# Sketched attention and a squared-ReLU FFN on one core: another order for the first batch, remainders of q through DRAM, k's outer products on GpSimd

## The chip, the cores and the metric

The kernel runs on one core of one Trainium2 chip. Its engines are TensorE (PE, with its weight loads PEld), VectorE (DVE), ScalarE (ACT), GpSimd (POOL) and SyncE (SP, which issues DMAs only). The metric is the device time of one execution in microseconds, as a median of several runs.

## The reference

Attention with polynomial sketched features, without a softmax, and then a feed-forward block with a squared ReLU on its output:

```python
# q, k, v: (4, 4, 1088, 32) float32; S1, S2: (8, 32)
def phi(x):
    a = np.einsum('rd,bhsd->bhsr', S1, x)
    b = np.einsum('rd,bhsd->bhsr', S2, x)
    return np.einsum('bhsi,bhsj->bhsij', a, b).reshape(*x.shape[:-1], 64)
q_p, k_p = phi(q), phi(k)
kv = np.einsum('bhsf,bhsd->bhfd', k_p, v)
z = np.sum(k_p, axis=2)
num = np.einsum('bhsf,bhfd->bhsd', q_p, kv)
den = np.einsum('bhsf,bhf->bhs', q_p, z)[..., None] + 1e-06
x = (num / den).transpose(0, 2, 1, 3).reshape(4352, 128)
h = np.maximum(x @ w_in, 0.0)            # w_in: (128, 2048)
out = h * h @ w_out                      # w_out: (2048, 128)
```

## The kernel before

There are four batches (`b`) of 1088 tokens and four heads. A batch is cut into two groups (`g`) of 512 tokens and a remainder of 64. The tokens of a group become one chunk of the FFN (8 chunks of 512 tokens); the remainders of all four batches together are the ninth chunk, of 256 tokens. For each chunk, the hidden size 2048 is taken in 16 blocks. A block is one product `pg` (f16, line 857), a ReLU into `gt`, a square into `g2`, and one product into `po` (f32, line 944). `first_product` (line 843) makes the first half up to three blocks ahead, `block` (line 923) does the second. The ReLU is done by DVE and the square by ACT (lines 873 and 876), or the ReLU by ACT and the square by GpSimd (lines 864 and 865), or both by ACT (lines 870 and 871); `first_product` chooses by counters.

The order of all instructions is written out by hand. The attention of a batch is cut into Python generators ("lanes") that `pump` (line 797) advances between blocks; `now` counts blocks. Counters such as `pool_free`, `quiet` and `ms_until` say from which block on an engine or a PSUM bank is taken to be free. When a chunk is asked for that isn't there yet, `first_product` sets `hurry` and drives all lanes until it is.

For a batch b >= 1, `batch_gen` (line 665) transposes k and q on DVE (`turned`), projects them on TensorE (`proj_rests`, `proj4`), and has the outer products `ph_k` of k's two factors made (`outer`, line 314): in two steps, group 0 on DVE, group 1 on GpSimd, then the remainder's on GpSimd (`outer_rest`). `KvRows` sums k's features against v, `spread` puts the sums into `kvbd`. The features of q take another way: the factors `qf` are stored to a DRAM scratch (`q_rows`) and read back by DMAs that repeat rows (`factors_gen`, line 272), and one GpSimd multiplication of two such tiles `f` gives the transposed features `phT` (line 300). `x_gen` (line 639) makes the numerators and denominators of a group (`numerators`, into the two PSUM banks of `nd`, each group of 256 columns filled up to 132), normalizes them on DVE, transposes the result on TensorE (`x_ps`) and copies it as the chunk `xT`. `second_gen` (line 720) does the second group.

For the remainder of q, GpSimd makes the outer products `phr_q`, TensorE transposes them (`rest_features_t`, line 748, `tr_ps`), and `rest_numerators` (line 762) makes their numerators in a bank of its own (`ndr`). `rest_x` (line 773) normalizes the remainders of two batches at a time.

Batch 0 is done ahead of the first block, from line 953 on. Its q features are transposed on TensorE (`feature_t`): those of group 0 before the first block, those of group 1 (`phq1`, outer products on DVE at line 1003) after the first two `pg`; group 1's numerators come from the lane `first_gen`. `idle_products` are matrix products of zeros into an unused bank. `sum_constants` (line 206) makes small constants on DVE. v comes in four DMAs per batch, each for 32 partitions and all four heads (`load_v`, line 110).

The last chunk is stored from two PSUM tiles by rows (`rows_store`, line 911), with four DMAs each on SP and ACT in turn; the products of the second tile's last three blocks are held back until the first is stored.

Of the kernel before, what the change touches and what calls it, by code (L numbers as in the profile page):

```python
# [21 lines left out]
def kernel(  # L22
# [19 lines left out]
    E = 128  # L42
# [67 lines left out]
    def load_v(b, i, eng):  # L110
        eng.dma_start(
            _v(v_sb[b], 0, [[256, H], [1, 256]], 32 * i, 32),
            bass.AP(
                v.tensor,
                v.offset + (b * H * S + 8 * i) * D,
                [[NM * D, 32], [S * D, H], [1, 256]],
            ),
        )
# [87 lines left out]
    def sum_constants():  # L206
        dve.tensor_reduce(
            out=pick_s[:, :], in_=_v(iden, 0, [[1, 32], [32, 4]]), axis=AX, op=add
        )
        dve.tensor_copy(  # L210
            out=_v(pick, 0, [[8, 32], [1, 8]]), in_=_v(pick_s, 0, [[1, 32], [0, 8]])
        )
        dve.tensor_reduce(
            out=_v(own_j, 0, [[8, 2], [1, 8]]),
            in_=_v(iden, 0, [[64, 2], [1, 8], [8, 8]]),
            axis=AX,
            op=add,
        )
# [53 lines left out]
    def factors_gen(b, qf, phT):  # L272
# [5 lines left out]
        for g in range(2):  # L278
            for pr in range(2):
# [16 lines left out]
                phT[g].append(fs)  # L296

# [33 lines left out]
    rest_ab = {}  # L331
    for r in range(2):
        rest_ab[r] = (
            cpool.tile([128, 128], F32, name=f"abr{r}"),
            {x: cpool.tile([128, 256], F32, name=f"phr_{x}{r}") for x in "kq"},
        )

    def proj_rests(items, ps_tag="ms"):

        ab_ps = pspool.tile([128, 128], F32, name="abr_ps", tag=ps_tag, bufs=2)  # L340
        for xt, b, kind in items:
            tiled(ab_ps, 64 * "kq".index(kind), 64, xt, 0, w_bd[:, :], 64, 64 * (b % 2))
        for xt, b, kind in items:
            p0, x = 64 * (b % 2), "kq".index(kind)
            if kind == "q" and any(y[1:] == (b, "k") for y in items):
                continue
            m = 8 if any(y[1:] == (b, "q") for y in items) and kind == "k" else 4
            act.copy(
                _v(rest_ab[b // 2][0], 32 * x, [[64, 2], [8, m], [1, 8]], p0, 64),
                _v(ab_ps, 64 * x, [[8, 2], [16, m], [1, 8]], p0, 64),  # L350
            )

    def outer_rest(b, kind, eng):
        p0, c0 = 64 * (b % 2), 32 * "kq".index(kind)
        ab, ph = rest_ab[b // 2]
        eng.tensor_tensor(
            out=_v(ph[kind], 0, [[64, 4], [8, 8], [1, 8]], p0, 64),
            in0=_v(ab, c0, [[8, 4], [1, 8], [0, 8]], p0, 64),
            in1=_v(ab, c0 + 64, [[8, 4], [0, 8], [1, 8]], p0, 64),
# [3 lines left out]
    class Kv:  # L363
# [25 lines left out]
        def rest(self):  # L389
            r, p0 = self.b // 2, 64 * (self.b % 2)  # L390
            self.products(rest_ab[r][1]["k"], 0, v_rm[r], 0, D, H * D, p0, 64)
# [10 lines left out]
    class KvRows:  # L402
# [26 lines left out]
        def products(self, phs):  # L429
# [11 lines left out]
            self.values(rest_ab[r][1]["k"], 0, v_rm[r], 0, D, p0, 64, False, True)  # L441
            self.factors(rest_ab[r][0], 0, 64, 0, p0, 64, False, True)
# [69 lines left out]
    def normalize(nd, T, xT, col, parts=1):  # L512
# [61 lines left out]
        for i in range(0, T, m):  # L574
            ms_used()
            x_ps = pspool.tile([128, 512], F16, name="x_ps", tag="ms", bufs=2)
# [34 lines left out]
    wanted = [-9]  # L611
    shared = [0]

    def pool_time(blocks):

        pool_free[0] = max(pool_free[0], now[0] + 0.7) + blocks
        return int(pool_free[0] - now[0]) + 1

# [20 lines left out]
    def x_gen(b, g, phT, rests=()):  # L639

        yield from take_nd()
        while pool_free[0] > now[0] + 0.6 and not hurry[0]:
            yield 1, 0
        nd = numerators(b, phT)
# [4 lines left out]
        yield next(norm)  # L649
        yield next(norm)  # L650
        next(norm)
        yield 1, 0
        nd_taken[0] = False
        for u in rests:
            rest_numerators(u)
        yield 1, 0
# [8 lines left out]
    def batch_gen(b):  # L665
# [3 lines left out]
        for x, sb in (("k", k_sb), ("q", q_sb)):  # L669
            if x == "q":  # L670
                yield from not_before(4 if b == 1 else n0 - 39)
            for g in range(2):
                xt[x, g] = turned(sb[b], g)
                yield 1, 1
        rests = [(turned(sb[b], 2), b, x) for x, sb in (("k", k_sb), ("q", q_sb))]
        if b == 1:
            rests.append((turned(q_sb[0], 2), 0, "q"))
        yield 1, 0
        yield from not_before(n0 - 28)
# [6 lines left out]
        lanes.insert(0, [factors_gen(b, qf, phT), now[0] + 1, 0])  # L686
        n1 = now[0]
        wanted[0] = n1 + 8
# [3 lines left out]
        for t0 in (0, 2):  # L692
            outer(phk[0], ab_k, t0, 2, dve, None, 0)
            outer(phk[1], ab_k, t0, 2, pool, None, 1)
            pool_time(1.0)
            yield 1, 1
        yield from pool_ready(1.0)
        outer_rest(b, "k", pool)
# [3 lines left out]
        while now[0] < ready and not hurry[0]:  # L702
# [10 lines left out]
            [second_gen(b, phT, n1, [x[1] for x in rests if x[2] == "q"]), n1 + 10, 0]  # L713
# [6 lines left out]
    def second_gen(b, phT, n1, rests):  # L720
        for u in rests:
            yield from pool_ready(1.0)
            outer_rest(u, "q", pool)
            pool_time(0.6)
            yield 1, 0
        yield from pool_ready(0)
        yield from ms_both()
        for u in rests:
            rest_features_t(u)
        yield 1, 0  # L730
        while 2 * b not in chunks:
            yield 1, 0
        yield from features_gen(b, phT, 1, n1 + 14)
        yield 1, 0
# [3 lines left out]

    def first_gen(phT):
        yield from x_gen(0, 1, phT)  # L740
# [7 lines left out]
    def rest_features_t(b):  # L748
        p0 = 64 * (b % 2)
        ph = rest_ab[b // 2][1]["q"]  # L750
        ms_used()
        t_ps = pspool.tile([128, 512], F32, name="tr_ps", tag="ms", bufs=2)
        for pr in range(2):
            nc.tensor.transpose(
                t_ps[:, 64 * pr : 64 * pr + 64],
                ph[p0 : p0 + 64, 128 * pr : 128 * pr + 128],
                iden[p0 : p0 + 64, p0 : p0 + 64],
            )
        phT_rem[b] = apool.tile([128, 128], F32, name="phTr", tag="phTr", bufs=2)
        act.copy(phT_rem[b][:, :], t_ps[:, 0:128])  # L760

    def rest_numerators(b):
        p0 = 64 * (b % 2)
        ms_used()
        nd = pspool.tile([128, 512], F32, name="ndr", tag="ms", bufs=2)
        for pr in range(2):
            tiled(
                nd, 2 * VW * pr, 2 * VW, phT_rem[b], 64 * pr,
                kvbd[b][:, 2 * VW * pr : 2 * VW * pr + 2 * VW], 64, p0,
            )  # L770
        act.copy(nd_rem[b // 2][p0 : p0 + 64, :], nd[p0 : p0 + 64, 0 : 4 * VW])

    def rest_x(r):
        beta = yield from normalize(nd_rem[r], 1, xT_rem, 128 * r)
        rem_beta.append((beta, 1))
        for w in range(2):
            for i in range(2):
                dst = bass.AP(
                    out.tensor,
                    out.offset + ((2 * r + w) * S + 32 + i) * E,  # L780
                    [[NM * E, 32], [1, E]],
                )
                rem_dst.append((dst, 64 * w + 32 * i, 32, 128 * r, 128))
# [30 lines left out]
    def store_gen(po, nt, betas, dsts):  # L814
# [7 lines left out]
        for t in range(T):  # L822
            nc.tensor.transpose(  # L823
                o_ps[:, 128 * t : 128 * t + 128], oT[:, 128 * t : 128 * t + 128], iden[:, :]
            )
        o_sb = fpool.tile([128, 512], F32, tag="o_sb", bufs=2)
# [16 lines left out]
    def first_product():  # L843
# [16 lines left out]
        calm = now[0] >= quiet[0] and not wanted[0] - 2 <= now[0] <= wanted[0] + 1  # L860
# [8 lines left out]
        elif now[0] == quiet[0] - 2 and nt == 512:  # L869
            act.activation(gt[:, 0:nt], pg[:, 0:nt], Relu)  # L870
            act.activation(g2[:, 0:nt], gt[:, 0:nt], Square)
        else:
            dve.tensor_scalar(  # L873
# [37 lines left out]
    def rows_store(r, ci):  # L911
# [8 lines left out]
        for i, (dst, p0, n, _, w) in enumerate(chunks[ci][3][4 * r : 4 * r + 4]):  # L920
            (sp, act)[i % 2].dma_start(dst, _v(o_sb, 0, [[1, w]], p0, n))

    def block():
# [6 lines left out]
        if nt < 512:  # L930
# [3 lines left out]
            if c < NC - 3:  # L934
# [34 lines left out]
    proj_rests([(xk[2], 0, "k")])  # L969
    phk = [ph_tile("ph_k", 3) for g in range(2)]  # L970
# [4 lines left out]
    xq = turned(q_sb[0], 0)  # L975
    idle_products(4)
    pq = proj(xq)
    outer_rest(0, "k", dve)
# [88 lines left out]
```

## Time and profile before

| what | value |
|---|---|
| median of 3 runs | 202.36 us (202.26 to 202.84) |
| the profiled execution | 202.01 us, of which the span is 200.2 us |
| granted TensorE clock | 0.998 |
| first `pg` starts | 17.86 us |
| a block without other work, start to start of `pg` | 1.07 to 1.08 us |
| DVE ReLU, 128x512 (L873) | 0.685 us, x92 |
| ACT square, 128x512 (L876) | 0.630 us, x92 |
| GpSimd square, 128x512 (L865) | 1.041 us, x27 |
| k's outer product 128x512, DVE / GpSimd in b >= 1 (L321) | 1.04 us / 1.27 us |
| GpSimd multiplication of q's factors (L300) | 1.276 us, x12 |
| remainder's outer product of q, GpSimd (L356) | 0.624 us, x4 |

All times below are of the one profiled execution, in microseconds from the start of its span. A row of the timeline gives start, length, engine, line, operation and tiles; in brackets stands how long the engine was idle before it and what released it. Rows that follow each other on one engine and line are merged (x2). In the chain of waits each piece is what held up the next, back from the last instruction. Matrix products are pipelined, so TensorE counts as busy across short waits; the starts of the `pg` products show them better than its busy share.

### The profile page before, as it was taken

How to read it: one execution, taken by the hardware profiler on the slowest of the kernel's cores; microseconds unless marked ns; L12 is line 12 of the kernel's file. 1: busy time of each engine (PE TensorE's matmuls, PEld its weight loads, DVE VectorE, ACT ScalarE, POOL GpSimd, SP SyncE). 2: the span in 40 equal slices, each digit the busy share in tenths (PEclk: the TensorE clock that was granted, in tenths of full speed). 3: DMA queues.
4: the chain of work that ended last, by engine and by line, in shares of the span. 5: the costliest groups of instructions: out<-in, count | busy, mean ns of one | idle time of the engine just before them, and what ended most of it. 6: DMA issues, size and time to landing. Idle time of an engine off the chain costs nothing.

```text
span 200.2 us, 3760 instructions
## 1 busy us (share of the span) xinstructions
PE 193.0 (96%) x1416; PEld 102.8 (51%) x1416; DVE 121.9 (61%) x271; ACT 109.4 (55%) x216; POOL 62.7 (31%) x82
## 2 busy tenths in 40 slices
PE   7798999999999999999999999999999999999992
PEld 2575455455445464564346555454455444444792
DVE  4768694644994717459966573648456844544671
ACT  2236757544565566354674554555647565565570
POOL 3502220844262207441262254331332222223000
PEclk9999999999999999999999999999999999999999
DMA  5999720488300245782000117501000200100021
GB/s 159 279 356 246 229 47 0 137 188 211 111 0 0 66 153 164 210 246 81 2 3 0 52 58 222 194 3 54 0 0 3 52 0 0 38 16 0 3 52 26
DMA packets 14994, 18.34 MB, mean 92 GB/s; under 512 B 3072, under 2 KB 9472, under 8 KB 14976
## 3 DMA queue, kind: packets, MB, share of 16 engines
q1 hardware_dynamic: 14416, 18.00, 32.1%
q8 instruction: 11, 0.18, 0.4%
q10 hardware_dynamic: 560, 0.11, 0.3%
q14 instruction: 7, 0.06, 0.1%
HBM read 15.08 MB, written 3.01 MB: 90 GB/s over the span
## 4 chain that ended last, share of the span: by engine, by line
PE 86%; DVE 6%; DMA 4%; issue 1%; ACT 1%; SPq 0%; DVEq 0%
PE po L944 50%; PE pg L857 15%; PE nd L245 5%; DVE gt L873 2%; DMA v_sb<-in_v_dram 2%; PE kvr_ps L412 2%; PE o_ps L823 2%; PE ab_ps L245 2%; DMA k_sb<-in_k_dram 2%; PE po_r L903 2%; PE po L903 2%; PE idle_ps L224 1%; PE ab_ps L262 1%; PE kv_ps L375 1%; DVE ph_k L321 1%
## 5 line engine op out<-in xcount | busy, mean ns | idle before, releaser
L944 PE MATMUL po<-g,w_o 128*128 128x512 f32 x256 | 130.7, 592 | 0.0
L873 DVE TENSOR_SCALAR gt<-pg 128x512 f32<-128x512 f32 (+1 forms) x108 | 69.1, 646 | 51.7 <-PE pg L857 40.5
L876 ACT ACTIVATE g<-gt 128x512 f32<-128x512 f32 (+1 forms) x108 | 64.2, 599 | 66.0 <-DVE gt L873 63.7
L944 PEld LDWEIGHTS po<-g,w_o 128*128 128x128 f32 x256 | 48.5, 191 | 35.6 <-issue 21.3
L865 POOL TENSOR_TENSOR g<-gt 128x512 f32<-128x512 f32 x27 | 28.1, 1041 | 79.7 <-ACT gt L864 79.5
L857 PE MATMUL pg<-xT,w_in 128*128 128x512 f16 x126 | 47.8, 381 | 0.6 <-DVE gt L873 0.6
L857 PEld LDWEIGHTS <-w_in 128*128 128x128 f16 x142 | 13.9, 98 | 24.0 <-issue 22.8
L300 POOL TENSOR_TENSOR phT<-f,f 128x512 f32<-128x512 f32 x12 | 15.2, 1276 | 8.2 <-DMA f<-q_rows 8.2
L864 ACT ACTIVATE gt<-pg 128x512 f32<-128x512 f32 x27 | 15.9, 588 | 0.0
L321 POOL TENSOR_TENSOR ph_k<-ab 128x512 f32<-128x512 f32 x8 | 9.7, 1236 | 5.9 <-ACT ab L269 4.7
L245 PEld LDWEIGHTS nd<-kvbd,phT 128*64 128x64 f32 x256 | 8.3, 137 | 5.3 <-issue 4.0
L321 DVE TENSOR_TENSOR ph_k<-ab 128x512 f32<-128x512 f32 x6 | 6.2, 1036 | 6.5 <-ACT ab L269 6.5
L245 PE MATMUL nd<-kvbd,phT 128*64 128x66 f32 x256 | 9.5, 225 | 0.2 <-ACT phT L72 0.2
L569 POOL TENSOR_TENSOR beta<-mp 128x4 f32<-128x4 f32 (+1 forms) x10 | 2.1, 206 | 21.0 <-DVE mp L539 21.0
L224 PE MATMUL idle_ps<-zero 128*128 128x512 f16 x23 | 7.1, 455 | 1.2 <-DVE own L185 1.2
L829 DVE TENSOR_TENSOR o_sb<-o_ps,beta 128x512 f32<-128x512 f32 x8 | 5.5, 692 | 4.5 <-PE o_ps L823 2.7
L245 PEld LDWEIGHTS ab_ps<-w_bd,xt 128*64 128x64 f32 x160 | 6.2, 139 | 3.0 <-DVE xt L234 1.5
L245 PE MATMUL ab_ps<-w_bd,xt 128*64 128x64 f32 x160 | 6.4, 225 | 0.8 <-DVE xt L234 0.7
L234 DVE STREAM_TRANSPOSE xt<-k_sb 128x512 f32<-128x512 f32 x8 | 5.5, 698 | 1.7 <-DMA k_sb<-in_k_dram 1.7
L903 PE MATMUL po<-w_o,g 128*128 128x128 f32 x32 | 6.2, 280 | 0.1
L823 PEld LDWEIGHTS o_ps<-iden,oT 128*128 128x128 f32 x32 | 4.0, 141 | 3.7 <-issue 2.9
L903 PE MATMUL po_r<-w_o,g 128*128 128x128 f32 x32 | 5.9, 275 | 0.0
(110 smaller groups left out, 150.8 us busy)
## 6 DMA issues: line engine op xcount, KB each, us to landing
f<-q_rows SPq DMA_DIRECT2D x12, 256.0 KB
f<-q_rows SPq DMA_DIRECT2D x24, 128.0 KB
v_sb<-in_v_dram SPq DMA_DIRECT2D x16, 128.0 KB
out_dram<-o_sb SPq DMA_DIRECT2D x32, 64.0 KB
k_sb<-in_k_dram SPq DMA_DIRECT2D x3, 544.0 KB
q_sb<-in_q_dram SPq DMA_DIRECT2D x3, 544.0 KB
w_in<-in_moe_w_in_dram SPq DMA_DIRECT2D x2, 512.0 KB
w_o<-in_moe_w_out_dram SPq DMA_DIRECT2D x2, 512.0 KB
```

The costliest lines, as they stand in the source:

```text
L224: nc.tensor.matmul(idle_ps[:, :], zero[:, 0:128], zero[:, :])
L245: nc.tensor.matmul(out_ps[p0 + c : p0 + c + z, c0 : c0 + w], lhsT[:, l0 + c : l0 + c + z], rhs)
L300: eng.tensor_tensor(out=sb[:, :], in0=fs[0][:, :], in1=fs[1][:, :], op=mult)
L321: eng.tensor_tensor(out=_v(ph, 256 * t0, [[64, 4 * m], [8, 8], [1, 8]]), in0=_v(a, c0, [[n, 4 * m], [1, 8], [0, 8]]), in1=_v(b, c1, [[n, 4 ...
L823: nc.tensor.transpose(o_ps[:, 128 * t : 128 * t + 128], oT[:, 128 * t : 128 * t + 128], iden[:, :])
L857: nc.tensor.matmul(pg[:, 0:nt], w_in[:, 128 * c : 128 * c + 128], xT[:, 0:nt])
L864: act.activation(gt[:, 0:nt], pg[:, 0:nt], Relu)
L865: pool.tensor_tensor(out=g2[:, 0:nt], in0=gt[:, 0:nt], in1=gt[:, 0:nt], op=mult)
L873: dve.tensor_scalar(out=gt[:, 0:nt], in0=pg[:, 0:nt], scalar1=0.0, scalar2=None, op0=amax)
L876: act.activation(g2[:, 0:nt], gt[:, 0:nt], Square)
L903: nc.tensor.matmul(po[r][:, 0:128], g2[:, 128 * r : 128 * r + 128], w_o[:, 128 * c : 128 * c + 128], start=c == 0, stop=c == NC - 1,)
L944: nc.tensor.matmul(po[0][:, 0:nt], w_o[:, 128 * c : 128 * c + 128], g2[:, 0:nt], start=(c == 0), stop=(c == NC - 1),)
```

## The change

The changed kernel computes the same result. In words:

- v comes in one DMA per head over all 128 partitions, four per batch as before.
- Before the first block: `xq` is transposed on DVE ahead of k's outer products, `xq1` after the sums of k; q's group 1 has its outer products on GpSimd, its transposes among the idle products ahead of the first `pg`, its copies on ACT and DVE, and its numerators directly behind the first two `pg`. `x_ps` of the first chunk is taken from the banks of `po`.
- `sum_constants` becomes a lane that starts at block 8, one of its three operations on GpSimd.
- For b >= 1, all four outer products of k are made on GpSimd.
- The remainder of q is projected with the roles of the operands swapped, stored to DRAM (`qr_rows`) and read back in six DMAs; GpSimd multiplies the two tiles. Transposes on TensorE and outer products on GpSimd go. Batch 1 carries two remainders, batches 2 and 3 one each.
- The remainder's numerators go into free columns of the second group's `nd`, ahead of that group's normalization.
- A counter `dve_free` is kept for DVE; transposes, normalization and stores wait in the order until it allows them, and ReLUs go to ACT when it is far ahead. GpSimd takes no squares until nine blocks after the projections (`held_until`). `pump` advances up to nine lanes per block instead of two.
- The last chunk's rows are stored with two DMAs per tile instead of four, and two blocks' products are held back instead of three.

```diff
@@ load_v
         eng.dma_start(
-            _v(v_sb[b], 0, [[256, H], [1, 256]], 32 * i, 32),
+            _v(v_sb[b], 256 * i, [[1, 256]]),
             bass.AP(
                 v.tensor,
-                v.offset + (b * H * S + 8 * i) * D,
-                [[NM * D, 32], [S * D, H], [1, 256]],
+                v.offset + (b * H + i) * S * D,
+                [[256, 4], [NM * D, 32], [1, 256]],
...
@@ factors_gen
                 phT[g].append(fs)
+        for u in fr:
+            yield from rest_factors_gen(u, fr[u])
...
@@ proj_rests
-            tiled(ab_ps, 64 * "kq".index(kind), 64, xt, 0, w_bd[:, :], 64, 64 * (b % 2))
+            p0 = 64 * (b % 2)
+            if kind == "k":
+                tiled(ab_ps, 0, 64, xt, 0, w_bd[:, :], 64, p0)
+            else:
+                nc.tensor.matmul(ab_ps[p0 : p0 + 64, 64:128], w_bt[:, :], xt[:, 0:64])
...
+                act.copy(rest_qf[b // 2][p0 : p0 + 64, :], ab_ps[p0 : p0 + 64, 64:128])
+
+    def rest_factors_gen(b, fs):
+
+        p0 = 64 * (b % 2)
+        rows = dpool.tile([64, 64], F32, name=f"qr_rows{b}", tag=f"qr_rows{b}")
+        sp.dma_start(rows[:, :], rest_qf[b // 2][p0 : p0 + 64, :])
+        yield 1, 0
+        for x in range(2):
+            f = apool.tile([128, 128], F32, name=f"fr{x}", tag=f"fr{x}", bufs=2)
+            for pr in range(2):
+                r0 = rows.offset + 64 * (32 * x + 16 * pr)
+                c = slice(64 * pr, 64 * pr + 64)
+                if x == 0:
+                    sp.dma_start(
+                        f[:, c], bass.AP(rows.tensor, r0, [[64, 16], [0, 8], [1, 64]])
+                    )
+                else:
+                    for h in range(2):
+                        sp.dma_start(
+                            f[64 * h : 64 * h + 64, c],
+                            bass.AP(rows.tensor, r0 + 512 * h, [[0, 8], [64, 8], [1, 64]]),
+                        )
+                yield 1, 0
+            fs.append(f)
+
+    def rest_features(b, fs):
+        phT_rem[b] = apool.tile([128, 128], F32, name="phTr", tag="phTr", bufs=2)
+        pool.tensor_tensor(
+            out=phT_rem[b][:, :], in0=fs[0][:, :], in1=fs[1][:, :], op=mult
+        )
...
+    def dve_time(blocks):
+
+        dve_free[0] = max(dve_free[0], now[0] + 0.2) + blocks
+
+    def dve_ready(slack):
+        while dve_free[0] > now[0] + slack and not hurry[0]:
+            yield 1, 0
...
@@ x_gen
-        yield from take_nd()
-        while pool_free[0] > now[0] + 0.6 and not hurry[0]:
-            yield 1, 0
-        nd = numerators(b, phT)
+        if nd is None:
+            yield from take_nd()
+            while pool_free[0] > now[0] + 0.3 and not hurry[0]:
+                yield 1, 0
+            nd = numerators(b, phT)
+            for u in rests:
+                rest_numerators(u, nd)
...
         yield next(norm)
+        dve_time(1.0)
+        yield from dve_ready(1.2)
         yield next(norm)
+        dve_time(0.8)
+        yield from dve_ready(1.2)
         next(norm)
+        dve_time(0.65)
...
@@ batch_gen
-            outer(phk[0], ab_k, t0, 2, dve, None, 0)
-            outer(phk[1], ab_k, t0, 2, pool, None, 1)
-            pool_time(1.0)
-            yield 1, 1
+            for g in range(2):
+                yield from pool_ready(1.0)
+                outer(phk[g], ab_k, t0, 2, pool, None, g)
+                pool_time(1.0)
+                yield 1, 0
...
@@ second_gen
-        for u in rests:
-            yield from pool_ready(1.0)
-            outer_rest(u, "q", pool)
-            pool_time(0.6)
-            yield 1, 0
-        yield from pool_ready(0)
-        yield from ms_both()
-        for u in rests:
-            rest_features_t(u)
...
         yield from features_gen(b, phT, 1, n1 + 14)
+        for u in rests:
+            yield from pool_ready(1.0)
+            rest_features(u, fr[u])
+            pool_time(0.5)
...
@@ first_product
-        calm = now[0] >= quiet[0] and not wanted[0] - 2 <= now[0] <= wanted[0] + 1
+        calm = now[0] >= quiet[0] and now[0] > held_until[0]
...
-        elif now[0] == quiet[0] - 2 and nt == 512:
+        elif (now[0] == quiet[0] - 2 or dve_free[0] > now[0] + 1.3) and nt == 512:
...
@@ block, rows_store
-            if c < NC - 3:
+            if c < NC - 2:
...
-        for i, (dst, p0, n, _, w) in enumerate(chunks[ci][3][4 * r : 4 * r + 4]):
-            (sp, act)[i % 2].dma_start(dst, _v(o_sb, 0, [[1, w]], p0, n))
+        for i, (dst, p0, n) in enumerate(chunks[ci][3][2 * r : 2 * r + 2]):
+            (sp, act)[i % 2].dma_start(dst, _v(o_sb, 0, [[1, 128]], p0, n))
...
@@ before the first block
+    xq = turned(q_sb[0], 0)
     phk = [ph_tile("ph_k", 3) for g in range(2)]
...
-    xq = turned(q_sb[0], 0)
-    idle_products(4)
+    idle_products(1)
     pq = proj(xq)
...
     pq1 = proj(xq1, "pg")
     phq1 = ph_tile("ph_q", 2)
+    for t0 in (0, 2):
+        outer(phq1, pq1[1], t0, 2, pool)
+    nd0 = numerators(0, pqT, True)
...
-    idle_products(12)
+    for t0 in (0, 2):
+        idle_products((4, 3)[t0 // 2])
+        for pr in range(2):
+            for t in (t0, t0 + 1):
+                nc.tensor.transpose(
...
+    act.copy(pqT1[0][:, :], tq1[0][:, :])
...
-    for t0 in (0, 2):
-        outer(phq1, pq1[1], t0, 2, dve)
+    dve.tensor_copy(out=pqT1[1][:, :], in_=tq1[1][:, :])
...
     first_two()
-    pqT1 = [feature_t(phq1, 4, pr, None) for pr in range(2)]
+    nd1 = numerators(0, pqT1, True)
+    nd_taken[0] = True
...
-    lanes.append([first_gen([x[0] for x in pqT1]), 3, 1])
+    lanes.append([x_gen(0, 1, None, (), nd1), 3, 1])
+    lanes.append([sum_constants(), 8, 0])
...
-        pump(2)
+        pump(9)
```

## The prediction, made before the changed kernel ran

> **What bounds the kernel now.** I read the page's busy shares first, then the chain that ended last in order of time, then the starts of the first products (`pg`) on TensorE, one per block, and last the rows around each place where two starts stand more than a block apart.
>
> ```profile
> PE 193.0 (96%) x1416; PEld 102.8 (51%) x1416; DVE 121.9 (61%) x271; ACT 109.4 (55%) x216; POOL 62.7 (31%) x82
> ...
> PE 86%; DVE 6%; DMA 4%; issue 1%; ACT 1%; SPq 0%; DVEq 0%
> ...
> 4.70 4.07 DMA v_sb<-in_v_dram
> 8.90 2.46 PE kv_ps L375 x72
> ...
> 17.86 0.59 PE pg L886 x2
> 18.45 0.87 PE t_ps L490 x8
> ...
> 22.96 1.09 PE nd L245 x32
> ...
> 56.23 0.38 PE L857 MATMUL pg<-xT,w_in 128*128 128x512 f16 x1
> 57.40 0.34 PE L754 MATMUL tr_ps<-iden,phr_q 64*128 64x64 f32 x4
> 57.67 0.39 PE L857 MATMUL pg<-xT,w_in 128*128 128x512 f16 x1
> ...
> 92.62 0.62 POOL L356 TENSOR_TENSOR phr_q<-abr 64x256 f32<-64x256 f32 x1
> 92.64 0.64 DVE L545 TENSOR_TENSOR small<-small,rm 128x16 f32<-128x16 f32 x1
> ...
> 117.15 2.54 POOL L321 TENSOR_TENSOR ph_k<-ab 128x512 f32<-128x512 f32 x2 [4.73 <-ACT ab L269]
> 117.22 1.54 DVE L321 TENSOR_TENSOR ph_k<-ab 128x512 f32<-128x512 f32 x1
> ...
> 196.45 1.71 SPq L921 DMA_DIRECT2D out_dram<-o_row  x4
> ```
>
> The first lines are the engines' busy shares and the chain's; rows from the chain follow (start, length, work), then rows of the timeline, one pair or triple for each kind of loss that the change touches. From 17.86 on TensorE is the bound: an undisturbed block is 1.075 us from one `pg` to the next (0.215 for `pg`, 0.86 for `po`), and 128 of them are 137.6 us. All other TensorE work in between is paid in full, so work taken off TensorE after 17.86 is worth its own length, and work off another engine only what TensorE really waits for it. Before 17.86 a chain through DMA, DVE and ACT sets the time; after the last product the stores do.
>
> **The change, part by part** (against the profiled execution's own 202.01 us).
>
> *Group 1 of batch 0.* Its eight transposes (0.87) lie between the first and the second pair of `pg`, while DVE and ACT make the first `g2`; its numerators (1.09 at 22.96) are paid later. The change does the transposes before the first `pg`, where TensorE now runs idle products (2.69), and puts the numerators where the transposes were. The later 1.09 goes; the filler is 0.22 longer, but the third pair of `pg` now waits 0.20 there (1.49 between starts, 1.29 of work). I take −1.0, between 0 (operands late) and −1.1.
>
> *Remainders of q.* The blocks with `tr_ps` last 1.44, 1.43 and 1.43 us: 3 x 0.36 = −1.1 (b = 1, 2, 3). The blocks with `ndr` last 1.56, 1.55 and 1.55: 1.44 over three plain ones. Their 16 products come back inside the `nd` groups at 1.09 / 32 = 0.034 each, 0.55. So −0.9. ACT loses four copies of 0.26 and gains four like the 0.21 of a 64x64 one; GpSimd loses four outer products of 0.62 and gains four multiplications 128x128, unseen, between the 0.24 of a small copy and 0.62.
>
> *DVE's part of the k outer products.* Six, 1.04 us each, go to GpSimd at 1.27. TensorE waits for DVE in two places: 96.35 to 99.33 (the remainder's normalisation of batches 0 and 1 among the transposes for batch 2), 0.66 + 0.12; and 118.28 to 120.89 (outer products on both engines), 0.07 + 0.40. The second goes with the outer products, the first by the new pacing (`dve_time`). Together 1.2, which I take; bound 0. GpSimd's own 4 x 1.27 + 0.63 = 5.7 us is hidden: it ends 6 us after `ab`, and the multiplications of `f` start only 43.02 − 35.17 = 7.9 after it, held by a DMA. If that cover goes, the 2.5 us by which the sums of k come later are paid.
>
> *v's loads.* The chain waits for `v_sb` until 8.90. The DMA engines are full there, yet move 265, 208 and 262 GB/s in the microseconds from 5.5 on, against 373 from 9.5. The 0.52 MB at 240 take 2.2 us; at 300 (the better k and q stretches) 1.75; at 373, 1.4. One load per head over 128 partitions instead of one per 32 partitions is seen nowhere. I take −0.6; ends 0 and −1.5, where DVE's first k outer product (some 7.3) would bind. The rest of the start follows: `xq` ahead of the outer products brings `ph_q` 0.5 before 10.13, and GpSimd's two q outer products (2.09 as the first pair) end by about 15.1, before the 16.06 at which the first half of `xs` is made. [...]
>
> *The end.* Four stores per row half become two, on both queues: the last issue ended at 196.45 + 1.80 on ACT; with two of 0.45 each, and `po_r` two products (0.22) earlier, it ends near 197.4. That is −0.85; I take −0.8, no less than the −0.2 of the products. The landing behind it (about 2 us) stays.
>
> *What is added.* Seven DMA issues per remainder on SP, 28 in all. The rows beside them are 0.55 and 0.58 each, so 4 us, and 2.06 passes between `q_rows` and the first load that reads it (34.71 to 36.77). Batch 1 has two remainders: SP ends its `f` issues at 45.3 and has four stores (1.7 to 3.4); then 2 x (0.4 + 2.1 + 3.4) end near 59 and land near 61. GpSimd's multiplication waits for that, and behind it in its queue stand squares (L865) and the second group's numerators, now at 62.14, which the new order puts two or three blocks later but the savings ahead two earlier. Cost 0 to 2. The normalisation of the remainders of batches 0 and 1 (L532, L545, L552, all reading two SBUF tiles) may fall on GpSimd's four k outer products; the pair at 92.6 shows 0.64 instead of 0.17. Three such waits of at most 1.27 are 3.8 on DVE, and some 2 of them pass the three blocks of look-ahead. Cost 0 to 2. Taken together I put +1.2. `sum_constants` costs nothing: 0.72 of DVE among the first blocks, where DVE idles 1.74 ahead of 24.48; `pqT1`'s copy on DVE (0.69) takes the place of an outer product of 0.68.
>
> Sum: −1.0 − 1.1 − 0.9 − 1.2 − 0.6 − 0.8 + 1.2 = −4.4, so 197.6 for a profiled run. The median of the runs is 0.35 above its profiled execution: **198.0**.
>
> **Rivals.**
>
> *Most of it given back in new waits.* Both costs at their upper ends (+4), v no earlier: −5.0 + 4.0 = −1.0 at worst, about −2.1 in the middle: 200.3 (199.4 to 201.7). For it: the lengthened rows at 92.64 and 117.22, and SP's tight end. Against: one DVE wait is covered by look-ahead. [...]
>
> *Slower: a chunk misses its block.* In the old order batch 1's projections come before `pg` number 11 and its first chunk is ready five blocks before its first product is due. By the new pacing the four transposes share DVE with the first normalisation, and I count the projections three blocks later and the normalisation one or two longer: none or two blocks left. If one more is lost, the kernel rushes that chunk: numerators, normalisation and transposes stand one behind the other, as 48.53 to 56.23 now, 7.7 us, with three blocks (3.2) of look-ahead to cover it: 4.5 lost, and the second group and the next transposes are pushed after it, about 1.5 more. −4.4 + 6.0 = +1.6: 204.0. Point of decision: `xT` of batch 1 later than 17 blocks behind its projections.
>
> [...]
>
> **Chances.** The forecast 0.58 (its own range 195.8 to 199.4: v at its good end and no waits is −6.5; the costs at two thirds is −3), given back 0.20, chunk missed 0.16, no effect 0.06. A measurement of this kernel can tell 0.3%, 0.6 us, from no change. Faster 0.78, same 0.06, slower 0.16. The range reaches over the second case and the last to 202.4; what is left out is the missed chunk and a little below 195.8.
>
> **What would show it.** Right: no `tr_ps` and `ndr`; the second numerators right behind the first pair of `pg`; the first `pg` 0.6 before 17.86; no gap over 0.1 near the old 98 and 119; the last store's issue 0.8 nearer to the last product. Wrong: GpSimd waiting for the remainders' factors with numerators behind it; DVE's L532 or L552 over 0.5 us beside an outer product; a gap of microseconds ahead of chunk 2.

## Result, and the profile after

The changed kernel takes 208.63 us (median of 4 runs, 207.24 to 210.06), the kernel before 202.45 in the same comparison: a ratio of 1.0303 (95% interval 1.0213 to 1.0394). It is 3% slower; the forecast was 198.0. The profiled execution took 207.52, of which the span is 205.7, against 202.01 and 200.2. Medians in this document are over all executions of a kernel, while ratios and their intervals leave out executions over 1.5% above its fastest: three of ten in `after_old_v` (the others have a median of 202.44) and in `old_v_and_stores`, two of six in `after_32_outermost`.

The page of the changed kernel: the engines' busy shares, TensorE's granted clock and the DMA engines' busy share in 40 slices of 5.1 us, and the shares of the chain that ended last.

```profile
PE 193.7 (94%) x1402; PEld 105.4 (51%) x1402; DVE 116.4 (57%) x262; ACT 113.2 (55%) x221; POOL 62.6 (30%) x85
...
PEclk9958999999999999999999999999999999999998
DMA  6697831048611044573410117612000100100200
...
PE 77%; DMA 14%; SPq 5%; issue 1%; ACT 0%; POOL 0%; DVE 0%
```

DVE lost 5.5 us of work, as meant. But DMA's share of the chain went from 4% to 14%, SyncE's queue appears in it with 5%, and the clock falls in the third and fourth slice. Before, it was full throughout:

```profile
PEclk9999999999999999999999999999999999999999
```

The chain of waits of the changed kernel (start, length, work):

```profile
4.87 6.83 DMA v_sb<-in_v_dram
...
11.74 4.08 PE kv_ps L414 x66
...
23.14 0.59 PE pg L932 x2
...
51.34 6.47 DMA qr_rows<-qfr
...
61.63 1.73 DMA qr_rows<-qfr
...
66.51 2.02 DMA fr<-qr_rows
...
68.60 0.46 POOL phTr L388
...
69.10 0.45 PE nd L247 x4
69.55 0.32 PE pg L902
```

Against the rows of before, the last piece of `v_sb` ends at 11.70 instead of 8.76, the sums of k (`kv_ps`) take 4.08 instead of 2.46, and the first `pg` comes at 23.14 instead of 17.86. In the middle a chain of stores and loads of the remainder's factors holds up TensorE; before, no DMA stood in the chain between 40 and 80.

The changed kernel by windows: length, busy time of each engine, then granted clock, DMA share, GB/s.

```profile
6.00:7.00 1.00, 1.00 (x15) 0.70 (x11) 0.51 (x1) 0.52 (x3) 0.76 (x1) 1.00 0.30 99
...
10.00:11.00 1.00, 0.47 (x2) 0.29 (x2) 0.00 (x0) 0.00 (x0) 0.00 (x0) 0.53 0.64 175
11.00:12.00 1.00, 0.26 (x4) 0.26 (x6) 0.00 (x0) 0.00 (x0) 0.00 (x0) 0.50 0.94 305
...
201.00:202.00 1.00, 0.00 (x0) 0.00 (x0) 0.00 (x0) 0.00 (x0) 0.00 (x0) 1.00 0.13 37
```

The same of the kernel before, while its loads of v are in flight and at its end:

```profile
5.50:6.50 1.00, 1.00 (x20) 0.81 (x21) 0.72 (x2) 0.60 (x3) 0.61 (x1) 1.00 1.14 265
...
197.00:198.00 1.00, 0.00 (x0) 0.00 (x0) 0.09 (x1) 0.00 (x0) 0.00 (x0) 1.00 0.25 66
```

In the microsecond from 6 to 7, when the new loads of v have the DMA engines almost to themselves, these are 30% busy and move 99 GB/s; the old loads kept them full. Counted by packet, the 512 packets of 1 KB that make up v take 4.3 of 16 engines all the way from 5.5 to 10.5, and the last ends at 11.28; before, it ended at 7.96. One such packet takes 48 ns of an engine now and 64 before: no engine works slower, but few of them work. While the new last stores are in flight, 0.13 to 0.14 of the engines are busy (some 2 of 16), where the old stores had 0.25.

The difference of the two profiled executions, 5.51, splits at the first and the last `pg` (17.86 and 194.29 before, 23.14 and 197.54 after): the start +5.28, the blocks −2.03 (176.43 to 174.40), the end +2.25. Both losses lie outside the blocks. Inside them the interval around batch 1's second numerators, with two remainders, is 4.72 instead of the 2.48 and 2.50 that the same blocks of batches 2 and 3 take with one: 2.24 more. Without it the blocks gained 4.27.

### The profile page after: what moved, and what is told of

Read it like the earlier page. It is cut to its first block, busy times and chain, and to the rows that moved or that the text cites. A ratio compares the mean times of both kernels' runs of the same rounds, so it can differ in the third digit from the quotient of the medians.

```text
span 205.7 us, 3767 instructions
## 1 busy us (share of the span) xinstructions
PE 193.7 (94%) x1402; PEld 105.4 (51%) x1402; DVE 116.4 (57%) x262; ACT 113.2 (55%) x221; POOL 62.6 (30%) x85
## 4 chain that ended last, share of the span: by engine, by line
PE 77%; DMA 14%; SPq 5%; issue 1%; ACT 0%; POOL 0%; DVE 0%
PE po L990 45%; PE pg L902 13%; DMA qr_rows<-qfr 4%; PE nd L247 4%; DMA v_sb<-in_v_dram 3%; DMA f<-q_rows 3%; SPq L379 2%; PE kv_ps L414 2%; PE po L949 2%; PE ab_ps L247 2%; PE po_r L949 2%; PE o_ps L866 2%; DMA k_sb<-in_k_dram 1%; PE kvr_ps L451 1%; PE ab_ps L264 1%; PE x_ps L617 1%
## 5 line engine op out<-in xcount | busy, mean ns | idle before, releaser
L910 POOL TENSOR_TENSOR g<-gt 128x512 f32<-128x512 f32 x21 | 21.8, 1039 | 80.9 <-ACT gt L909 80.9
L325 POOL TENSOR_TENSOR ph_k<-ab 128x512 f32<-128x512 f32 x14 | 14.5, 1070 | 11.9 <-ACT ab L271 10.5
L909 ACT ACTIVATE gt<-pg 128x512 f32<-128x512 f32 x21 | 12.3, 584 | 0.2
L916 ACT ACTIVATE g<-gt 128x512 f32<-128x512 f32 x14 | 8.8, 630 | 0.6
L915 ACT ACTIVATE gt<-pg 128x512 f32<-128x512 f32 x14 | 8.2, 585 | 0.0
L247 PEld LDWEIGHTS ab_ps<-w_bd,xt 128*64 128x64 f32 x160 | 6.7, 155 | 2.3 <-issue 1.2
L226 PE MATMUL idle_ps<-zero 128*128 128x512 f16 x17 | 6.4, 483 | 1.2 <-DVE own L185 1.2
L236 DVE STREAM_TRANSPOSE xt<-q_sb 128x512 f32<-128x512 f32 x8 | 5.4, 696 | 3.3 <-DMA q_sb<-in_q_dram 3.3
L247 PE MATMUL ab_ps<-w_bd,xt 128*64 128x64 f32 x160 | 6.9, 242 | 0.1
L414 PE MATMUL kv_ps<-v_sb,ph_k 128*64 128x64 f32 x64 | 4.6, 312 | 2.4 <-DMA v_sb<-in_v_dram 2.4
```

The lines of the kernel that those rows point to most:

```text
L236: dve.transpose(xt[:, :], _v(x, 128 * g, [[32, 4], [256, 4], [1, 32]]))
L247: nc.tensor.matmul(out_ps[p0 + c : p0 + c + z, c0 : c0 + w], lhsT[:, l0 + c : l0 + c + z], rhs)
L325: eng.tensor_tensor(out=_v(ph, 256 * t0, [[64, 4 * m], [8, 8], [1, 8]]), in0=_v(a, c0, [[n, 4 * m], [1, 8], [0, 8]]), in1=_v(b, c1, [[n, 4 ...
L910: pool.tensor_tensor(out=g2[:, 0:nt], in0=gt[:, 0:nt], in1=gt[:, 0:nt], op=mult)
```

## Experiments

The theory after this reading, A: the two rewritten transfers run on few DMA engines, because of the order of the dimensions in their patterns.

**One part undone or done alone.** `after_old_v` is the changed kernel with the old load of v:

```diff
-                [[256, 4], [NM * D, 32], [1, 256]],
+                [[NM * D, 32], [S * D, H], [1, 256]],
```

> The changed kernel with one thing undone: v comes again in four DMAs of 32 partitions and all heads (32 outermost). Theory A (the source pattern of the new load has 4 as its outermost size, so that it runs on few DMA engines and lands late): kv starts near 8.9 as in the kernel before, not 11.74; the clock stays at 1.0 until then or nearly; the first pg is at 17.4 to 18.3 instead of 23.14, and the time falls by 4.8 to 5.7 us, to about 202. Rival B (the removed idle products let the clock fall, and that costs the start): kv may start earlier, but the clock still falls to 0.5, kv takes about 4 us again, and the first pg stays above 19.5; the time falls by less than 3.6.

Measured: 203.28, ratio 1.0002 (0.9977 to 1.0027). The clock is full at the start and the sums of k take 2.46, so rival B is out; but they begin at 9.53 and the first `pg` comes at 18.78, 0.5 later than expected. `after_old_stores`, the changed kernel with four last stores per tile:

```diff
-                [[E, 2], [NM * E, 32], [1, E]],
+                    [[NM * E, 32], [1, E]],
```

> The changed kernel with one thing undone: the last chunk's rows are stored with four DMAs of 32 rows per tile again instead of two of 64 rows whose outermost size is 2. Theory A (outermost size 2 means two DMA engines per store): from the last o_row to the end of the span 3.4 us as before or less instead of 5.9, the time falls by 2 to 2.9 us. Rival B (fewer stores are good, and the late end comes from something else, such as a busy memory): the end stays within 0.5 us of the changed kernel's, or gets 0.6 later for two more issues.

Measured: 206.39, ratio 1.0173 (1.0114 to 1.0233); the end comes 3.7 after the last output row instead of 5.6, not quite the 3.4 expected. `before_new_v` is the kernel before with the new load of v, the first diff the other way round:

> The kernel before with the new load of v alone (all batches). Theory A: kv starts at about 11.7 instead of 8.9 and TensorE idles longer ahead of it, so that the clock may fall as well; first pg between 20.6 (landing alone) and 22.5 (with a cold clock), time 205 to 207. Rival B (the order of the first batch in the changed kernel makes the loads late): kv still near 9 and the time within 0.6 us of the kernel before.

Measured: 207.96, ratio 1.0278 (1.0250 to 1.0307), 1.0 over the expected range; first `pg` at 22.16, at a clock that fell too (0.992 over the execution, 0.998 before). `before_new_stores`, the kernel before with two last stores per tile, the second diff the other way round:

> The kernel before with the two-DMA row stores alone (three products held back as before). Theory A: the last stores land 2 to 2.6 us later, time 204.2 to 205. Rival B (the prediction's step): the last issue ends 0.6 to 0.9 earlier and the time falls to about 201.7.

Measured: 204.93, ratio 1.0116 (1.0100 to 1.0132); 5.3 from the last row to the end, 3.1 before. So each rewritten transfer alone makes the kernel before slower, v by some 5.4 and the stores by 2.4, and each one undone takes most of its part away.

**The order of the dimensions.** These four leave open whether a transfer is slow for its order or for going to 128 partitions or from 64. `after_32_outermost` moves the same rows in the same transfers, in another order:

```diff
@@ load_v
-                [[256, 4], [NM * D, 32], [1, 256]],
+                [[NM * D, 32], [256, 4], [1, 256]],
@@ rest_x
-                [[E, 2], [NM * E, 32], [1, E]],
+                [[NM * E, 32], [E, 2], [1, E]],
```

> The changed kernel with the two outer dimensions of its new transfers swapped: the source pattern of each load of v has the dimension of 32 outermost and that of 4 inside it, and the destination of each last store the 32 outside the 2. The same rows of 1 KB and 2 KB move in the same number of transfers, to and from as many partitions; rows of v reach other partitions, and the last rows of the output other places, than the reference has them. Theory A (the count of the outermost dimension sets how many DMA engines a transfer runs on): the products of k and v start at 8.5 to 9.9 and the first projection comes at 18 to 19.2 in place of 23.14, the last output row is followed by the end within 3.5 in place of 5.6, and the time is 200.4 to 203.5, level with or under the kernel before. Rival B (the new transfers are slow because each of them goes to 128 or from 64 partitions, or because there are fewer of them): the first projection stays at 22 to 23.5, the end at 5 or more behind the last row, and the time at 206 to 210.

It keeps the work and leaves out the right places: rows of v meet the wrong rows of k, and output rows change places, so its result isn't the reference's. A last store's row is 512 bytes (64 rows in 32 KB), not the 2 KB named above.

Measured: 200.73 (198.86 to 202.44), ratio 0.9853 (0.9811 to 0.9895). Its chain of waits:

```profile
2.36 3.98 DMA q_sb<-in_q_dram
...
8.13 2.71 PE kv_ps L414 x72
...
17.63 0.59 PE pg L932 x2
```

v is out of the chain: the sums of k start at 8.1, earlier than the 8.9 of the kernel before, and q is what the start waits for. The end comes 3.3 after the last row (195.21 to 198.5). Both are better than expected. Swapping the two outer dimensions in each of two patterns is worth some 8 us between the medians. So the order of the dimensions is shown to be the cause, and the count of partitions and of transfers is cleared; that it acts by the number of engines is read from the shares and the packets above: 4.3 of 16 engines for v's packets with 4 outermost, a share of 0.13 (2.1 of 16) for the last stores with 2. By what rule the size sets the number, no run here shows.

**Landing or clock.** `new_v_kept_warm` keeps TensorE busy with idle products while v is in flight:

```diff
     pq = proj(xq)
-    idle_products(1)
+    idle_products(14)
```

> The changed kernel with its new load of v, but more products on idle data ahead of the first real ones (14 in place of 1), so that TensorE doesn't stand idle while v is in flight. Nothing of the result depends on them. Theory A (the 5.28 us by which the first projection is late are the late landing, some 3.5, and a lowered clock behind it, some 1.7): the granted clock before 16.5 stays near 1.0, the products of k and v take 2.5 to 2.8 in place of 4.08, and the first projection comes at 21 to 21.8 in place of 23.14. Rival B (the lowered clock is not from idling, or the path goes through VectorE's work on q): the first projection stays within 0.5 of 23.14.

Measured, in one execution: 204.21, with the first `pg` at 21.63. TensorE's rows there:

```profile
7.61 3.19 PE L226 MATMUL idle_ps<-zero 128*128 128x512 f16 x14
10.73 0.45 PE L414 MATMUL kv_ps<-v_sb,ph_k 128*64 128x64 f32 x6
12.50 1.96 PE L414 MATMUL kv_ps<-v_sb,ph_k 128*64 128x64 f32 x58 [1.32 <-DMA v_sb<-in_v_dram]
```

v lands no earlier (0.8 later in this execution), but the 58 products take 1.96 (3.46 in the changed kernel, rows from 11.74) and the clock stays at 1.0. Of the 5.28 at the start, 1.5 is thus the lowered clock (23.14 to 21.63) and 4.0 the order of the pattern (21.63 to 17.63), by one execution each. From the 58 products on, the clock alone costs 2.3 (11.40 to the first `pg` against 9.13).

What is left, 17.86 to 17.63, is no gain of the new order of the first batch. From the end of the sums of k to the first `pg` it takes 6.78 or 6.79 in the six traces that have this order at full clock, up to `kept_warm` below, and 6.50 or 6.51 in the four with the old order. The sums end 0.5 earlier (10.85 against 11.36).

**Both undone, and the remainder's chain.** `old_v_and_stores` is the changed kernel with both of the first two diffs.

> The changed kernel with the old load of v and the old last stores of the remainders; the rest of the change stays. Theory A (both losses are the two rewritten transfers, each on few DMA engines, and the rest of the change is worth what its terms said): the first projection comes at 18.5 to 19, the time from the last output row to the end falls from 5.3 to 5.6 back to about 3.1, and the time is 199.5 to 200.5, 1.0 to 1.5 per cent under the kernel before (203.28 with the old v alone, less the 2.5 that the stores cost the kernel before). Rival B (the last rows come later with four stores, because the two issuing queues carry two stores each): the end gains under 1 and the time stays at 202.5 to 203.3, level with the kernel before.

Measured: 201.93 (200.38 to 203.73, 10 runs), ratio 0.9930 (0.9891 to 0.9968). It is spread over 3.3 us, and only its two quickest executions lie in the expected 199.5 to 200.5. By their mean granted clock the ten fall in two groups: five at 0.995 to 1.000 took 200.38 to 200.96, five at 0.986 to 0.992 took 202.90 to 203.73. Against 202.82 for the kernel before (202.16 to 203.23), only the first group is faster. The first `pg` comes at 19.21 and the end 3.7 after the last row, both later than expected. The profiled execution is one of the longest, 203.67. There the interval around batch 1's second numerators is 5.07, and by windows:

```profile
63.00:65.90 2.90, 0.78 (x15) 0.57 (x11) 0.00 (x0) 0.40 (x2) 0.45 (x1) 1.00 0.08 20
65.90:67.00 1.10, 1.10 (x4) 0.48 (x4) 0.61 (x2) 0.26 (x1) 0.00 (x0) 0.87 0.00 0
67.00:68.00 1.00, 1.00 (x3) 0.67 (x2) 0.96 (x4) 0.68 (x2) 0.00 (x0) 0.50 0.00 0
```

TensorE waits there, busy 0.78 of 2.90, and then runs at a clock of 0.50 until about 70: in this execution the wait is paid twice. The chain of waits of the changed kernel shows what it waits for: SyncE stores the first remainder's rows, waits for their landing, issues the loads, and only then stores the second remainder's rows and waits again. `rows_stored_early` stores both together with the other rows:

```diff
@@ factors_gen
         sp.dma_start(rows[:, :], qf[:, :])
+        rest_rows = {u: rest_rows_store(u) for u in fr}
         yield 1, 0
...
-            yield from rest_factors_gen(u, fr[u])
+            yield from rest_factors_gen(u, fr[u], rest_rows[u])
```

> As old_v_and_stores, and the remainders' q rows are stored to DRAM together with the other q rows, before the loads of the rows' features are issued, so that a landing no longer stands ahead of the second store. Theory A (the stall before batch 1's projections is the chain store, landing, load, landing on SyncE's queue): the 1.6 to 2.2 us that TensorE waits at the start of batch 1's second half are gone, VectorE's product of numerator and denominator there waits for nothing from GpSimd's multiply, and the time is 1.5 to 2.2 under old_v_and_stores, about 198.2. Rival B (GpSimd is late by its own work, the outer products): GpSimd's multiply starts no more than 0.5 earlier, and the time is within 0.5 of old_v_and_stores.

Measured: 199.96 (199.65 to 201.66, 4 runs), ratio 0.9876 (0.9832 to 0.9921). That is 2.0 under the median of `old_v_and_stores`, but part of it is the clock. The three executions at 0.998 or more took 199.65 to 200.21, some 0.8 under the first group there. The expected 198.2 wasn't reached. GpSimd's second multiplication of the remainders in the changed kernel, then rows of GpSimd and TensorE in `rows_stored_early`:

```profile
68.60 0.45 POOL L388 TENSOR_TENSOR phTr<-fr,fr 128x128 f32<-128x128 f32 x1 [3.71 <-DMA fr<-qr_rows]
```

```profile
60.38 0.47 POOL L391 TENSOR_TENSOR phTr<-fr,fr 128x128 f32<-128x128 f32 x1
61.31 0.46 POOL L391 TENSOR_TENSOR phTr<-fr,fr 128x128 f32<-128x128 f32 x1 [0.46 <-DMA fr<-qr_rows]
...
62.88 0.40 PE L247 MATMUL nd<-kvbd,phTr 128*64 128x66 f32 x4
63.73 0.42 PE L247 MATMUL nd<-kvbd,phTr 128*64 128x66 f32 x4 [0.45 <-ACT nd_rem L810]
```

The second multiplication waits 0.46 instead of 3.71, and the interval falls to 3.36. With the second store behind the first landing the interval was 3.88 to 5.33 in five traces and 3.35 in a sixth (`new_v_kept_warm`, where the first landing took 6.2 as well but the chain no longer ended last); with the rows stored early it is 3.35 or 3.36 in all four. So the old order of the stores doesn't always cost, and the new one never did here. Theory A holds with a correction: 0.88 over the 2.48 of batch 2 stays, and it is no DMA. The second remainder's products (0.42) wait 0.45 for ACT to copy the first one's out of the same columns.

**k's outer products.** `k_half_on_dve` is `rows_stored_early` with half of them on DVE again:

```diff
-            for g in range(2):
-                yield from pool_ready(1.0)
-                outer(phk[g], ab_k, t0, 2, pool, None, g)
+            yield from pool_ready(1.0)
+            outer(phk[0], ab_k, t0, 2, dve, None, 0)
+            dve_time(1.0)
+            outer(phk[1], ab_k, t0, 2, pool, None, 1)
```

> As rows_stored_early, but k's outer products are again half on VectorE and half on GpSimd, paced by the planner as in the kernel before. Theory A (the term of 1.2 in the prediction: moving them to GpSimd removed two waits of TensorE of 2.98 and 2.61 in the kernel before): the time rises by 0.3 to 1.2 over rows_stored_early, and gaps of TensorE over 1.1 us come back at some 95 and 115 us. Rival B (the gaps came from something else in the change, or VectorE's free time covers the outer products): within 0.3 of rows_stored_early, no such gap.

Measured: 200.90 (199.57 to 202.07), ratio 0.9884 (0.9827 to 0.9941), against 0.9876. The median is 0.94 over that of `rows_stored_early`, where theory A wanted 0.3 to 1.2. But from the first to the last `pg` it takes 172.92, `rows_stored_early` 173.03, and no wait of TensorE for DVE comes back among the blocks. Its profiled execution, 202.07, lost its time at the start, which the edit doesn't touch:

```profile
11.00:12.00 1.00, 1.00 (x24) 1.00 (x23) 0.49 (x1) 0.00 (x0) 0.00 (x0) 0.50 0.98 383
```

The clock is at 0.50 here, as in the changed kernel, and the sums of k take 4.01. The other long execution has a low clock too (201.88 at 0.988); the two at 0.995 and 0.998 took 199.57 and 199.92, no longer than `rows_stored_early` at such clocks. Rival B is right for the blocks: with the rest of the change in place, it doesn't matter where these products are made. `before_k_on_pool` does the move alone, in the kernel before (the diff the other way round, without `dve_time`):

> The kernel before with one part of the change alone: k's outer products of batches 1 to 3 all on GpSimd, each paced by the planner. Theory A (the prediction's term of 1.2, two waits of TensorE for VectorE's subtraction near 98 and 120 come from VectorE's share of these products): the two intervals of 1.19 and 1.47 there fall to 1.08, any other lengthening is under 0.3, and the time is 0.5 to 1.2 under the kernel before. Rival B (VectorE has room for its share, as the version with half of it on VectorE shows, and the waits come from the other work that fell together with it): the time is within 0.4 of the kernel before, with waits of the same size somewhere near there.

Measured: 202.55 (202.19 to 202.85), ratio 0.9982 (0.9958 to 1.0006): no difference that can be told. The wait near 119 is gone (0.46), but two other intervals grew by 0.27 together, and the wait near 98 is as before. Rows of GpSimd and DVE there:

```profile
97.41 1.04 POOL L866 TENSOR_TENSOR g<-gt 128x512 f32<-128x512 f32 x1 [3.06 <-ACT gt L865]
...
97.58 1.02 DVE L552 TENSOR_TENSOR xs<-nd_rem,small 128x128 f16<-128x128 f32 x1
98.52 0.68 DVE L874 TENSOR_SCALAR gt<-pg 128x512 f32<-128x512 f32 x1
```

The ReLU is queued behind the remainder's normalization, and the interval around it is 1.79, as before the edit. That normalization takes 1.02 beside a square of GpSimd; the same operation of the later batches, with GpSimd idle, takes 0.29 (158.47). So the wait near 98 comes from a square of GpSimd and not from DVE's outer products.

**A version that holds.** `kept_warm` is `rows_stored_early` with TensorE kept busy until v lands:

```diff
-    idle_products(1)
+    idle_products(4)
     pq = proj(xq)
-    idle_products(1)
+    idle_products(5)
```

> As rows_stored_early, with 9 products on idle data in place of 2 around q's projection, so that TensorE has work until v lands. Theory A (the spread of these kernels, 199.6 to 202.1, is the clock that falls to 0.5 in some executions while TensorE waits for v): the granted clock before 16 is 1.0 in the profiled execution, all executions lie within 0.8 of each other, and the median is 199.5 to 199.9. Rival B (the spread has another cause, later in the kernel): executions over 201 come as often as before, one in four or more.

Measured: 200.02 (199.85 to 200.27, 4 runs), ratio 0.9872 (0.9850 to 0.9895). The profiled execution has full clock at the start, and all runs lie within 0.42 at 0.995 or more, where the two kernels without it spread over 2.0 and 2.5; the median, at the level of `rows_stored_early`, is 0.1 above what was expected. Four runs are few for the absence of longer ones, though the four of the next kernel have none either. `outer_after_norm` takes one GpSimd operation out of the way of DVE; the transposes that read it, and their copies, move behind it:

```diff
+    outer(phq1, pq1[1], 0, 2, pool)
-    for t0 in (0, 2):
-        outer(phq1, pq1[1], t0, 2, pool)
...
     for _ in range(3):
         next(norm)
+    outer(phq1, pq1[1], 2, 2, pool)
```

> As kept_warm, with the second half of GpSimd's outer products of batch 0's group 1 after the normalization of group 0, and the transposes that read it behind the first transposes of x. Theory A (the 0.60 of VectorE's product of 128x16, 0.18 elsewhere, is a wait for GpSimd's outer product that runs beside it, and it lies on the path to the first projection): that product takes 0.18 to 0.25, the first projection comes 0.3 to 0.5 earlier after the end of the products of k and v, and the time is 0.2 to 0.5 under kept_warm. Rival B (the 0.42 is hidden, or the moved transposes take its place on the path): within 0.2 of kept_warm or slower.

Measured: 199.81 (199.27 to 200.20, 4 runs), ratio 0.9858 (0.9833 to 0.9882). One row of DVE in `kept_warm`, while GpSimd makes outer products (14.25 to 16.34), and the same row in `outer_after_norm`, with none beside it:

```profile
15.78 0.60 DVE L574 TENSOR_TENSOR small<-small,small 128x16 f32<-128x16 f32 x1
```

```profile
15.85 0.17 DVE L574 TENSOR_TENSOR small<-small,small 128x16 f32<-128x16 f32 x1
```

From the start of the sums of k to the first `pg` the path shortens from 9.25 to 8.83, nearly all of that 0.43. In the time it is 0.2 with overlapping ranges: theory A by the trace, not settled by the times alone. This kernel, the change with the old transfers and three small repairs, is 1.4% faster than the kernel before, and the fastest here that leaves the computation whole.

## Why the prediction was wrong

*v's loads*, −0.6, became +5.3 at the first `pg`. This is the step that failed first. The prediction priced the number of partitions that a load reaches and put its worst end at 0; it never looked at the order of the source pattern, where a 4 took the place of a 32. The outermost 4 cost 4.0 at the first `pg`. The other 1.5 is a cost that no term had: TensorE's clock, lowered while it waited (0.50 from 10.06 to 16.89). That a load gains by reaching more partitions, no run shows: with 128 of them and 32 outermost (`after_32_outermost`) the last packet of v ends at 8.08, no earlier than the 7.96 of before, though other traffic shared the engines. The sums of k do end 0.5 earlier there, near the predicted 0.6, but by another way: with one load per head, the first products need only the first load (in the changed kernel they begin in pairs, at 8.19, 9.11 and 10.36, and wait for v in between).

*The end*, −0.8, "no less than the −0.2 of the products", became +2.25. The products gave their part: from the last `pg` to the last row it is 2.57 instead of 2.80. The shorter issue gave next to nothing: the last issue ended 1.45 after that row's DVE operation began, and now 1.37, for it can't begin before the row is made and takes 0.76 on ACT, not 0.45. The landing, which "stays" at 2, became 4.5 (201.19 to 205.7). The same rows went out on fewer engines (a share of 0.13 to 0.14 in place of 0.25). With 32 outermost (`after_32_outermost`) the time from the last `pg` to the end is 5.89 against 5.93 before: the −0.8 wasn't there even without the slow landing. With four stores in the changed kernel (`rows_stored_early`) it is 6.26; why that is more than before stays open.

*What is added*, +1.2, was 2.24 in the changed kernel, one place, and named rightly: GpSimd waits for the remainder's factors with numerators behind it. The prediction had SyncE finish near 59; it finished at 67.1, of which 5.3 is the late start. The rest is the first landing. The prediction had counted two rounds of store, landing and loads, with 2.5 for a store and its landing. The second took 1.73, at a DMA share of 0.12; the first took 6.47, with loads still in flight (0.70 from 52 to 54). The other half of that term, DVE behind GpSimd's outer products, came as the prediction feared (the remainder's normalization took 1.06 beside one, from 84.45) but cost nothing among the blocks (1.08 from `pg` to `pg` there). It came at the start instead (0.42).

The price of 1.27 for a GpSimd outer product was the mean of two rows, 1.07 and 1.52; with DVE elsewhere four take 4.14 (40.53 to 44.67), and 4.85 with the remainder's, where 5.7 were counted.

*The four gains inside the blocks* were right: −1.0, −1.1, −0.9 and −1.2 are −4.2; measured from the intervals between `pg`, −1.07 (first eight blocks), −1.08 (three `tr_ps`), −0.76 (`ndr`, without the wait) and −1.22 (the two places of waiting), −4.13, and the blocks without the wait gained 4.27. Of the first, 0.28 is given back ahead of the first `pg` (6.50 to 6.78). The split of the 1.2 held too: the second place goes with the outer products (`before_k_on_pool`, 0.46), the first doesn't. That the new pacing is what removes the first wasn't tested alone. But with the rest of the change in place the move itself is worth nothing (`k_half_on_dve`).

*Rivals.* No chunk missed its block. "Given back in new waits" had the right mechanism in the middle of the kernel, at a size between the forecast's and its own, and was silent on both ends, where the time was lost. No rival let a rewritten transfer itself become slower: the price that the old rows show for a transfer was taken as the floor for the new one.

## What to carry to other kernels

When a DMA's pattern is rewritten, read the outermost size of both sides before anything else: its fall from 32 to 4 in v's loads cost the kernel before 5.4 us, and the fall from 32 to 2 in the last stores 2.4, though these were fewer and larger. Where several transfers depend on each other in one queue, issue all first steps before the first wait (GpSimd's wait for the second remainder fell from 3.71 to 0.46). TensorE's waits for the late v, 0.59, 0.92 and 0.91 in the changed kernel, cost 1.5 to 2.3 more in clock; so idle products belong across such waits, sized to the transfer (`kept_warm`, 0.995 or more in all four executions).

## What was not expected of the hardware

The granted clock fell to 0.50 where TensorE was thinly used for about 3 us (busy 0.78 of 2.90 in `old_v_and_stores`). In all five traces where it fell ahead of the last product it stayed there for 3.41 us or twice that, 6.83 (10.06 to 16.89 in the changed kernel), however busy TensorE was by then (4.00 of the 4.00 us from 12 on there); a wait of 1.32 with idle products ahead of it didn't lower it (`new_v_kept_warm`). Why the same start keeps full clock in one execution and not in the next, no run here shows.

GpSimd's outer product of 128x512 took 1.07 us where DVE was elsewhere, 1.51 to 1.57 where DVE's own had begun before it (`k_half_on_dve`), and where GpSimd began first (117.15 in the kernel before) it took 1.07 and DVE's took 1.54, against 0.69 with GpSimd idle (75.11 there): whichever came second took longer. The means of the table of the kernel before, 1.04 and 1.27, mix both cases.
